# One weight sum earlier and four token sums one round later, at the end of an attention and two-layer kernel

## The chip, the cores and the metric

The kernel runs on one core of one Trainium2 chip. The metric is the device time of one execution in microseconds; the times given are medians over runs of the same program. TensorE (PE) multiplies, VectorE (DVE) and ScalarE (ACT) read its results out of the accumulator banks and work on them, GpSimd (POOL) masks and issues loads, SyncE (SP) issues stores and transposing transfers. Each engine takes its own instructions in the order in which the program lists them.

## What is computed

The reference first does causal attention, with 16 beacon keys and values ahead of the sequence, and then a two-layer block with a leaky ReLU between:

```python
B, H, S, Nb, D = (8, 8, 576, 16, 64)
n_tokens, d_model, d_ff = (4608, 512, 2048)
...
scores = scale * np.matmul(q, k_all.transpose(0, 1, 3, 2))   # k_all: beacon_k, then k
scores = np.where(causal, -1000000000.0, scores)
a = np.exp(scores - scores.max(-1, keepdims=True))
a /= a.sum(-1, keepdims=True) + 1e-09
attn_out = np.matmul(a, v_all)
...
x = attn_out.transpose(0, 2, 1, 3).reshape(B * S, H * D)
h = x @ w_in
g = np.maximum(0.01 * h, h)
return (g @ w_out).astype(np.float32)
```

## The kernel before

**Tiling.** The 4608 tokens are nine chunks of 512, numbered 0 to 8. The first layer of a chunk makes 16 blocks of 128 features (`up`, through `moe1`, line 442: four matmuls of 128x512 into one bank, then one ACT activation, line 450, into `gT`). The second layer is made by `down` (line 544). From chunk 1 on it is split in seven products over quarters of the operands instead of eight (Strassen's scheme in Winograd's form): products 1, 4, 6, 2, 7, 5, 3 in this order, each in two `down` steps of eight matmuls of 128x256. Products 5, 6 and 3 need sums over `gT`, which `token_sums` lists: four DVE additions for every four features, s1, s2, the overwritten quarter a21, and s4. DVE does them in `add_due` (line 784).

**The last two chunks.** When attention runs out of work, chunks 7 and 8 make a part of their first layer by seven products too. `in_round` makes four of the 16 blocks: products 1, 2, 6, 5, 4, 7, 3 (line 663, four matmuls of 128x256 each), with one `down` of the chunk behind it after product 1, after 5 and after 3. Product 1 and product 2 share a bank: ACT copies it after product 1 (line 697, called the p1 copy here), and product 2 then adds into the same bank. ACT copies product 5 in the same way (line 709). DVE combines (lines 706, 717, 718, 720, 721), and three activations, the leaves (line 680), wait in the list `leaves` for the results of lines 718, 720 and 721. `leave_all` issues them in the next round, one after its p1 copy, one after its product 2, one after its product 5, or all at once where it is called without a number. Weight sums for these products (`w_in_sums`) and sums over the tokens' columns (`x_in_sums`) are DVE work also.

**What sets the order.** The order is written out by hand. Nothing moves an instruction on its engine except the order in which the code calls it. DVE's sums go through a list, `due`: `add_due()` takes one off the front, and `up` and `down` each call it once. What a step leaves in the list is done at a later step. At the end of the attention part the list holds the rest of the weight sums and the token sums of chunk 6. `last_chunks` then takes the steps of a string one by one. `D` puts the list aside, does two `down`s and puts the list back. `X31` turns the last head pair, `x7` and `x8` make the column sums (two at once, two into the list at its third place), `R111` is an `in_round` with three `down`s, `t` issues all leaves and lists the token sums of the first four features, `u` is `leave_all` and `up`, `d` is `down`, `w` lists the last weight sums.

The steps for chunk 7 are `D X31 x7 d a1 R111 x8 R111 t u d u d u d u u d u d u u w`, those for chunk 8 `R111 R111 t R111 u d u d u d u d d d14`.

**Buffers.** The accumulators of the rounds and of `up` rotate through four banks (`ps_one`, named acc), those of `down` in this stage through two (`ps_sc`, named sc).

Of the kernel before, what the change touches and what calls it, by code (L numbers as in the profile page):

```python
# [15 lines left out]
def kernel(  # L16
# [383 lines left out]
    def x_transposes(g, copy):  # L400
        b, hp = divmod(g, NPAIR)
        x_nat, _ = xs.pop(g)
        ps = ps_one.tile([128, 1024], BF16, name="tp", tag="one")
        for t, (q0, rows) in enumerate(QT):
            nc.tensor.transpose(
                ps[:, q0 : q0 + rows],
                x_nat[0:rows, t].rearrange("p e d -> p (e d)"),
                ident[0:rows, 0:rows],
            )
        copy(out=xT[:, hp, x_at(b) : x_at(b) + S], in_=ps[:, 0:S])  # L410
# [20 lines left out]
    def moe1(i, fc):  # L431
        if i not in gT:
            gT[i] = gpool.tile([128, NF, 512], BF16, name="gT")
        acc = ps_one.tile([128, 512], FP32, name="acc", tag="one")
        at = i * 512 % (XR * S)
        cut = min(512, XR * S - at)
        for lo, hi in ((0, cut), (cut, 512)):
            for j in range(NJ):
                if lo == hi:
                    continue  # L440
                x0 = (at + lo) % (XR * S)
                nc.tensor.matmul(  # L442
                    out=acc[:, lo:hi],
                    lhsT=w_in_cols(fc, j),
                    rhs=xT[:, j, x0 : x0 + hi - lo],
                    start=(j == 0),
                    stop=(j == NJ - 1),
                    skip_group_check=True,
                )
        nc.scalar.activation(out=gT[i][:, fc, :], in_=acc, func=AF.Prelu, alpha=0.01)  # L450
# [25 lines left out]
    def token_sums(i, lo, hi):  # L476
        if i not in sums:
            sums[i] = [sum_tile(n).rearrange("p (c t) -> p c t", c=HF) for n in range(3)]
        g, s = gT[i], sums[i]
        a11, a12 = g[:, lo:hi, 0:HT], g[:, HF + lo : HF + hi, 0:HT]  # L480
        a21, a22 = g[:, lo:hi, HT : 2 * HT], g[:, HF + lo : HF + hi, HT : 2 * HT]
        s1, s2, s4 = (s[n][:, lo:hi] for n in range(3))
        return [
            dict(out=s1, in0=a21, in1=a22, op=ADD),
            dict(out=s2, in0=s1, in1=a11, op=SUB),
            dict(out=a21, in0=a11, in1=a21, op=SUB),
            dict(out=s4, in0=a12, in1=s2, op=SUB),
        ]
# [70 lines left out]
    def add_late(now=False):  # L559
        while late and (now or late[0][0] < done1[0] + done2[0]):  # L560
            late.pop(0)[1]()
# [57 lines left out]
    def w_in_sums(n, lo=0, hi=ROUNDS, first=False):  # L619
        cols = slice(lo * 256, hi * 256)  # L620
        (b11, b21), (b12, b22) = (
            [w_in_sb[i][:, at : at + 2, cols] for at in (0, 2)] for i in range(2)
        )
        x, y = {5: (b12, b11), 6: (b22, w_t[5][:, :, cols]), 4: (b21, w_t[6][:, :, cols]), 7: (b22, b12)}[n]
        at = 0 if first else len(due)
        due[at:at] = [
            (TAIL - 1, dict(out=w_t[n][:, j, cols], in0=x[:, j], in1=y[:, j], op=SUB)) for j in range(2)
        ]
# [8 lines left out]
    def x_in_sums(i):  # L637
        (a11, a12), (a21, a22) = x_parts(i)
        s1, s2, s3, s4 = (
            flat_a[t][:, lo : lo + X_COLS].rearrange("p (j t) -> p j t", j=2)  # L640
            for t, lo in sum_at[4 * (i - TAIL) : 4 * (i - TAIL) + 4]
        )
        x_sums[i] = {5: s1, 6: s2, 7: s3, 3: s4}
        return [
            (i, dict(out=s1, in0=a21, in1=a22, op=ADD)),
            (i, dict(out=s2, in0=s1, in1=a11, op=SUB)),
            (i, dict(out=s4, in0=a12, in1=s2, op=SUB)),
            (i, dict(out=s3, in0=a11, in1=a21, op=SUB)),
        ]
# [24 lines left out]
    def leave_all(n=3):  # L674
        while leaves and n:
            leave(*leaves.pop(0))
            n -= 1
# [9 lines left out]
    def in_round(i, r, downs):  # L687
        if i not in gT:
            gT[i] = gpool.tile([128, NF, 512], BF16, name="gT")
        add = nc.vector.tensor_tensor  # L690

        def bank():
            return ps_one.tile([128, 512], FP32, name="acc", tag="one")

        one = bank()
        in_product(i, 1, r, one, True)
        nc.scalar.copy(out=temps["p1"], in_=one)
        leave_all(1)
        for _ in range(downs[0]):
            down()  # L700
        in_product(i, 2, r, one, False)
        leave(i, 2 * r, 0, one)
        leave_all(1)
        six = bank()
        in_product(i, 6, r, six, True)
        add(out=temps["u2"], in0=six, in1=temps["p1"], op=ADD)
        five = bank()
        in_product(i, 5, r, five, True)
        nc.scalar.copy(out=temps["p5"], in_=five)
        leave_all()  # L710
        for _ in range(downs[1]):
            down()
        four = bank()
        in_product(i, 4, r, four, True)
        seven = bank()
        in_product(i, 7, r, seven, True)
        add(out=temps["u3"], in0=seven, in1=temps["u2"], op=ADD)
        add(out=temps["c21"], in0=four, in1=temps["u3"], op=ADD)
        in_product(i, 3, r, five, False)
        add(out=temps["c12"], in0=five, in1=temps["u2"], op=ADD)  # L720
        add(out=temps["c22"], in0=temps["u3"], in1=temps["p5"], op=ADD)
        leaves.extend(((i, 2 * r, 1, temps["c21"]), (i, HF + 2 * r, 0, temps["c12"]), (i, HF + 2 * r, 1, temps["c22"])))
        for _ in range(downs[2]):
            down()
        done1[0] += 4

    def last_chunks(steps):
        for step in steps.split():
            op, n = step[0], int(step[1:] or 1)
            i = done1[0] // NF  # L730
            if op == "d":
                for _ in range(n):
                    down()
            elif op == "u":
                for _ in range(n):
                    leave_all()
                    up()
            elif op == "R":
                in_round(i, done1[0] % NF // 4, [int(x) for x in step[1:]])
            elif op == "X":  # L740
                x_transposes(n, nc.vector.tensor_copy)
            elif op == "w":
                w_in_sums(7, ROUNDS - 1, ROUNDS)
            elif op == "x":
                x = x_in_sums(n)
                if n == TAIL:
                    for _, op in x[:2]:
                        nc.vector.tensor_tensor(**op)
                    due[2:2] = [x[3], x[2]]
                else:  # L750
                    due.extend(x)
            elif op == "a":
                add_due(n)
            elif op == "D":
                later = due[:]
                due.clear()
                down()
                down()
                due.extend(later)
            elif op == "t":  # L760
                leave_all()
                due.extend((i, op) for op in token_sums(i, 0, SLICE))
# [19 lines left out]
    def add_due(n=1):  # L782
        while due and n:
            nc.vector.tensor_tensor(**due.pop(0)[1])  # L784
            n -= 1
# [7 lines left out]
    def up():  # L793
        i1, n = divmod(done1[0], NF)
        assert i1 < ready[0]
        add_late()
        fc = n if i1 == 0 else n // 2 + n % 2 * HF
        moe1(i1, fc)
        if (i1, n) == (TAIL - 1, 4 * (ROUNDS - 1) + 2):
            w_in_sums(7, 0, ROUNDS - 1, first=True)  # L800
        add_due()
        done1[0] += 1
        turn[0] = 1
        if i1 and n % (2 * SLICE) == 2 * SLICE - 1:
            due.extend((i1, op) for op in token_sums(i1, n // 2 + 1 - SLICE, n // 2 + 1))

    def down():
        add_late()
        add_due()
        if at2[1] == 4:  # L810
            add_all(at2[0])
        moe2(*at2)
        done2[0] += 1
        at2[1] += 1
        if at2[1] == ND(at2[0]):
            at2[:] = at2[0] + 1, 0
        turn[0] = 0
# [94 lines left out]
    with order:  # L912
# [93 lines left out]
        assert at2 == [TAIL - 1, ND(TAIL - 1) - LEFT] and done1[0] == TAIL * NF, (at2, done1)  # L1006
        apart_from_values[0] = True
        last_chunks("D X31 x7 d a1 R111 x8 R111 t u d u d u d u u d u d u u w")
        last_chunks("R111 R111 t R111 u d u d u d u d d d14")


# [28 lines left out]
```

## Time and profile before

| what | value |
|---|---|
| median of 3 runs | 327.86 us (326.22 to 327.97) |
| time of the profiled execution | 328.3 us |
| its span, first to last instruction | 326.2 us |
| granted TensorE clock | 1.000 |
| busy: PE, DVE, ACT, POOL | 314.7, 168.2, 204.3, 184.4 us |
| last group of masks on POOL | up to 247.6 us |
| the string for chunk 7 begins with its first `down` | at 257.4 us |
| the first round of chunk 8 begins | at 284.0 us |
| last 128 matmuls, all of `down` | from 308.7 us |

Times of instructions are us from the start of the span. A row of the timeline gives the start, the time for which the instructions of the row were busy, engine, line, what is written and what is read, and the count. In brackets stands how long the engine sat idle before and what it then waited for. A row of several matmuls ends later than the next one starts, since the end of a matmul overlaps the next; so the pace of PE is read from start to start. Eight matmuls of 128x256 take 0.87 us in that way.

### The profile page before, as it was taken

The page shows a single profiled execution, that of the slowest core. Times are in us where ns is not written, and L with a number is a line of the kernel's source. Part 1 is how long each engine was busy: PE and PEld are TensorE (multiplying, and loading weights), DVE is VectorE, ACT ScalarE, POOL GpSimd, SP SyncE. Part 2 cuts the span into 40 slices and gives each one's busy share as a digit, 9 for nine tenths or more (in the row PEclk, how much of TensorE's full clock was granted, in tenths as well). Part 3 has the DMA queues.
Part 4 walks back from the last instruction along what each step waited for, and adds up shares of the span by engine and source line. Part 5 has one row for each costly group of instructions (what it writes and reads, how often), then busy time and mean ns, then how long its engine had stood idle before and what let it go on. Part 6 is the DMA issues. An engine that isn't in the chain of part 4 may idle for free.

```text
span 326.2 us, 8700 instructions
## 1 busy us (share of the span) xinstructions
PE 314.7 (96%) x3468; PEld 218.9 (67%) x3494; DVE 168.2 (52%) x341; ACT 204.3 (63%) x346; POOL 184.4 (57%) x354
## 2 busy tenths in 40 slices
PE   7999999999999999999999999999999989998995
PEld 4575555445688558845888888646865777687784
DVE  3473245508356145434553455345454689577754
ACT  4968962488765786478647873786477446564510
POOL 8795868989997687659875977674221000000000
PEclk9999999999999999999999999999999999999999
DMA  8999999999999999999999999999112100200113
GB/s 132 133 195 187 127 215 135 167 156 213 142 146 167 220 136 123 104 191 71 143 173 193 110 131 110 194 135 124 52 52 81 23 2 32 98 1 2 64 66 129
DMA packets 155256, 39.78 MB, mean 122 GB/s; under 512 B 142368, under 2 KB 152480, under 8 KB 155216
## 3 DMA queue, kind: packets, MB, share of 16 engines
q0 software_dynamic: 99824, 18.54, 88.6%
q1 hardware_dynamic: 55120, 20.62, 37.4%
q8 instruction: 27, 0.44, 0.6%
q14 instruction: 13, 0.11, 0.1%
q10 hardware_dynamic: 272, 0.07, 0.1%
HBM read 37.22 MB, written 9.44 MB: 143 GB/s over the span
## 4 chain that ended last, share of the span: by engine, by line
PE 76%; DMA 13%; ACT 4%; POOL 3%; issue 1%; DVE 1%; SPq 0%; ACTq 0%; DVEq 0%
PE acc L442 25%; PE acc L544 19%; PE sc L544 11%; PE av L359 7%; PE sc L314 6%; DMA gsum<-in_k_dram 5%; PE acc L663 4%; DMA w_out_sb<-in_moe_w_out_dram 4%; DMA kT<-k_nat 3%; ACT aT L333 2%; DMA k_nat<-in_k_dram 2%; PE sc L267 1%; POOL aT L289 1%; PE av L823 1%; ACT aT L276 1%
## 5 line engine op out<-in xcount | busy, mean ns | idle before, releaser
L442 PE MATMUL acc<-xT,w_in_sb 128*128 128x512 bf16 (+1 forms) x537 | 116.5, 354 | 1.6 <-ACT aT L329 0.3
L450 ACT ACTIVATE gT<-acc 128x512 bf16<-128x512 f32 x124 | 70.9, 623 | 33.2 <-PE acc L442 32.6
L289 POOL TENSOR_SCALAR_AFFINE_SELECT aT<-aT 128x256 bf16<-128x256 bf16 (+2 forms) x160 | 59.5, 403 | 50.5 <-ACT aT L329 30.9
L442 PEld LDWEIGHTS <-w_in_sb 128*128 128x128 bf16 x560 | 51.7, 98 | 44.0 <-issue 3.0
L544 PEld LDWEIGHTS <-gT 128*128 128x128 bf16 x512 | 48.8, 98 | 7.6 <-issue 1.6
L333 ACT ACTIVATE aT<-sc 128x1024 bf16<-128x1024 f32 (+3 forms) x64 | 51.7, 891 | 0.0
L329 ACT ACTIVATE aT<-sc 128x512 bf16<-128x512 f32 (+3 forms) x64 | 29.0, 520 | 27.5 <-PE sc L314 26.7
L388 DVE RECIPROCAL rec<-av 128x6 f32<-128x6 f32 (+1 forms) x64 | 12.0, 187 | 64.5 <-PE av L359 63.9
L359 PEld LDWEIGHTS <-aT 128*128 128x128 bf16 (+1 forms) x960 | 36.9, 98 | 9.0 <-issue 1.0
L544 PEld LDWEIGHTS <-gsum 128*128 128x128 bf16 x384 | 36.4, 98 | 7.7 <-DVE gsum L784 1.2
L359 PE MATMUL av<-v_aug,aT 128*128 128x65 bf16 (+1 forms) x960 | 39.7, 194 | 0.7 <-POOL aT L289 0.3
L214 POOL DMA_DIRECT2D v_aug<-in_v_dram x40 | 34.2, 858 | 4.1 <-DMA w_in_sb<-in_moe_w_in_dram 3.5
L171 POOL DMA_DIRECT2D k_nat<-in_k_dram x48 | 34.8, 732 | 1.9 <-DMA q_nat<-in_q_dram 0.7
L171 POOL DMA_DIRECT2D q_nat<-in_q_dram x48 | 34.8, 730 | 0.5 <-issue 0.3
L389 DVE TENSOR_TENSOR x_nat<-av,rec 128x384 bf16<-128x384 f32 (+1 forms) x64 | 31.4, 491 | 2.2
L544 PE MATMUL acc<-w_out_sb,gT 128*128 128x256 bf16 x240 | 28.9, 273 | 0.4 <-ACT gT L450 0.4
L276 ACT ACTIVATE aT<-sc 128x1024 bf16<-128x1024 f32 (+3 forms) x32 | 25.9, 871 | 4.3 <-PE sc L267 2.2
L314 PE MATMUL sc<-qT,kT 64*128 64x80 bf16 (+22 forms) x384 | 22.1, 250 | 0.2 <-DMA kT<-k_nat 0.2
L314 PEld LDWEIGHTS <-kT 64*128 64x128 bf16 x384 | 12.7, 94 | 11.1 <-issue 7.7
L544 PE MATMUL acc<-w_sum,gsum 128*128 128x256 bf16 x160 | 20.1, 273 | 0.0
L575 ACT COPY p<-acc 128x512 f32<-128x512 f32 x15 | 9.1, 604 | 16.8 <-PE acc L544 16.8
L784 DVE TENSOR_TENSOR gsum<-gT 128x1024 bf16<-128x1024 bf16 x16 | 11.3, 704 | 16.0 <-ACT gT L450 16.0
(95 smaller groups left out, 339.7 us busy)
## 6 DMA issues: line engine op xcount, KB each, us to landing
out_dram<-p SPq DMA_DIRECT2D x26, 256.0 KB, 3.6
q_nat<-in_q_dram POOLq DMA_DIRECT2D x48, 72.0 KB, 5.6
k_nat<-in_k_dram POOLq DMA_DIRECT2D x48, 72.0 KB, 5.0
v_aug<-in_v_dram POOLq DMA_DIRECT2D x24, 128.0 KB, 6.6
w_in_sb<-in_moe_w_in_dram POOLq DMA_DIRECT2D x2, 1024.0 KB, 12.1
w_out_sb<-in_moe_w_out_dram POOLq DMA_DIRECT2D x2, 1024.0 KB, 12.2
out_dram<-u SPq DMA_DIRECT2D x8, 256.0 KB, 2.7
gsum<-in_q_dram POOLq DMA_DIRECT2D x8, 144.0 KB, 7.1
```

Of the source, the lines that this page charges most:

```text
L171: nc.gpsimd.dma_start(out=t[:, :, par], in_=(q, k)[which][b, 2 * hp + par].rearrange("(t p) d -> p t d", p=NR),)
L214: nc.gpsimd.dma_start(out=dst[lo : ROWS[c], c, :, 0:D], in_=v[b, :, OFF[c] : OFF[c] + n].rearrange("h p d -> p h d"),)
L276: nc.scalar.activation(out=aT[:, :, c0 : c0 + w], in_=sc[:, :, 0:w], func=AF.Exp, scale=0.125)
L289: nc.gpsimd.affine_select(out=view, in_=view, compare_op=ALU.is_ge, fill=0.0, base=128 - n if lo == 0 else 0, channel_multiplier=-1, patte ...
L314: nc.tensor.matmul(out=(sc[par] if apart else sc[:, par])[:, at : at + b - a], lhsT=kT[ps_, c * 128 : (c + 1) * 128], rhs=qT[ps_, q0 : q0 ...
L329: nc.scalar.activation(out=probs[g][:, par, lo:hi], in_=sc[par][:, at : at + hi - lo], func=AF.Exp, scale=0.125)
L333: nc.scalar.activation(out=probs[g][:, :, lo:hi], in_=sc[:, :, at : at + hi - lo], func=AF.Exp, scale=0.125)
L359: nc.tensor.matmul(out=avv[:, n, 0 : D + 1], lhsT=aT[0 : ROWS[c], par, a0 : a0 + 128], rhs=va[0 : ROWS[c], c, 2 * hp + par, :], start=(c = ...
L389: nc.vector.tensor_tensor(out=x_nat[:, t0:t1].rearrange("p t e d -> p (t e) d"), in0=avv[:, :, 0:D], in1=rec[:, n0:n1, None].to_broadcast( ...
L442: nc.tensor.matmul(out=acc[:, lo:hi], lhsT=w_in_cols(fc, j), rhs=xT[:, j, x0 : x0 + hi - lo], start=(j == 0), stop=(j == NJ - 1), skip_gro ...
L450: nc.scalar.activation(out=gT[i][:, fc, :], in_=acc, func=AF.Prelu, alpha=0.01)
L544: nc.tensor.matmul(out=acc[:, lo : lo + HD], lhsT=left(i, n, fc, tile), rhs=right(n, fc), start=(lo == 0 and fc == 0), stop=(fc == HF - 1) ...
```

## The change

Two places. Inside `up`, at one block of chunk 6 (the one whose call lists the weight sums for product 7 ahead of everything), two sums are taken off the list instead of one. In the string for chunk 8, `t` stands after the third round instead of after the second. An assertion states that the list which `D` puts aside has four entries.

```diff
             elif op == "D":
                 later = due[:]
+                assert len(later) == 4, len(later)
                 due.clear()
                 down()
                 down()
...
         if (i1, n) == (TAIL - 1, 4 * (ROUNDS - 1) + 2):
             w_in_sums(7, 0, ROUNDS - 1, first=True)
+            add_due()
         add_due()
...
         last_chunks("D X31 x7 d a1 R111 x8 R111 t u d u d u d u u d u d u u w")
-        last_chunks("R111 R111 t R111 u d u d u d u d d d14")
+        last_chunks("R111 R111 R111 t u d u d u d u d d d14")
```

## Prediction

> **What bounds the kernel.** I read first the busy times and the chain of work that ended last, then the waits of PE, then the busy time by stage.
>
> ```profile
> PE 314.7 (96%) x3468; PEld 218.9 (67%) x3494; DVE 168.2 (52%) x341; ACT 204.3 (63%) x346; POOL 184.4 (57%) x354
> ...
> PE 76%; DMA 13%; ACT 4%; POOL 3%; issue 1%; DVE 1%; SPq 0%; ACTq 0%; DVEq 0%
> ```
>
> PE is busy for 96% of the span and holds 76% of the chain. Only the end matters here, since the change touches nothing ahead of 250 us. The waits of PE from 240 us to the end are two in all (waiter, what it waited for, total, times, longest):
>
> ```profile
> PE acc L663 <- ACT kT L697: 1.3, 1, 1.3
> PE sc L544 <- DVE gsum L784: 0.9, 1, 0.9
> ```
>
> Elsewhere in those 86 us PE waits for nobody, at a granted clock of 1.00. So the end is set by PE's list of matmuls plus these two gaps. Both lie at what the diff touches.
>
> The first gap, PE and then DVE:
>
> ```profile
> 262.47 0.60 PE L663 MATMUL acc<-aT 128*128 128x256 bf16 x4
> 262.91 0.60 PE L544 MATMUL sc<-w_sum,gsum 128*128 128x256 bf16 x4
> 264.43 0.61 PE L544 MATMUL sc<-w_sum,gsum 128*128 128x256 bf16 x4 [0.92 <-DVE gsum L784]
> ```
>
> ```profile
> 260.56 0.42 DVE L748 TENSOR_TENSOR aT<-aT,xT 128x512 bf16<-128x512 bf16 x1
> 260.91 0.55 DVE L784 TENSOR_TENSOR aT<-w_in_sb,aT 128x768 bf16<-128x768 bf16 x1
> 261.38 0.68 DVE L784 TENSOR_TENSOR gsum<-gT 128x1024 bf16<-128x1024 bf16 x1
> 261.98 0.42 DVE L784 TENSOR_TENSOR aT<-xT 128x512 bf16<-128x512 bf16 x1
> 262.74 0.69 DVE L706 TENSOR_TENSOR kT<-acc,kT 128x512 f32<-128x512 f32 x1 [0.35 <-PE acc L663]
> 263.35 0.42 DVE L784 TENSOR_TENSOR aT<-xT,aT 128x512 bf16<-128x512 bf16 x1
> 263.69 0.69 DVE L784 TENSOR_TENSOR gsum<-gsum,gT 128x1024 bf16<-128x1024 bf16 x1
> ```
>
> Product 6 of chunk 6 has its first four operands, but the other four are s2 of the last features, which DVE makes at 263.69 to 264.38. Ahead of it stand a weight sum (260.91), s1 (261.38), two column sums and line 706, which itself waits for PE.
>
> The second gap, PE and then ACT, in the third round of chunk 8:
>
> ```profile
> 295.38 0.60 PE L663 MATMUL acc<-xT,w_in_sb 128*128 128x256 bf16 x4
> 295.81 1.04 PE L544 MATMUL sc<-w_out_sb,gT 128*128 128x256 bf16 x8
> 298.14 0.60 PE L663 MATMUL acc<-xT,w_in_sb 128*128 128x256 bf16 x4 [1.29 <-ACT kT L697]
> ```
>
> ```profile
> 295.79 0.63 ACT L680 ACTIVATE gT<-aT 128x512 bf16<-128x512 f32 x1 [1.84 <-DVE aT L718]
> 296.39 0.63 ACT L680 ACTIVATE gT<-kT 128x512 bf16<-128x512 f32 x1
> 296.99 0.63 ACT L680 ACTIVATE gT<-aT 128x512 bf16<-128x512 f32 x1
> 297.52 0.57 ACT L697 COPY kT<-acc 128x512 f32<-128x512 f32 x1
> ```
>
> Product 1 ends at 295.98, and its copy could start there. But `t` put the three leaves of the second round ahead of the copy, and the first of them waits for DVE until 295.79. The copy ends at 298.09, and product 2 starts at 298.14.
>
> **The change, part by part.** No matmul, activation, addition or transfer is added or taken away. The instruction order of the changed kernel shows PE's, POOL's and SP's lists unchanged. So every DMA issue keeps its place; only DVE and ACT are reordered.
>
> *The second `add_due` in `up`.* The second half of the product 7 weight sum (0.41 us, at 252.93) moves ahead of a reciprocal, and everything after it in the list moves up one step. What remains for `D` is four token sums instead of five entries, and the weight sum at 260.91 now runs right behind its other half, at about 256.2. The list after `x7` becomes s1, s2, column sum, line 706, column sum, a21, s4. From the rows: the second L748 starts at 260.56, s1 takes its place at 260.91, s2 follows after a pace of 0.60 at 261.51 and ends at 262.20. PE wants it at 262.91 + 0.44 = 263.35. The margin is 1.15 us, so the gap goes. From start to start PE took 264.43 - 262.91 = 1.52 us for what takes 0.44: **1.08 us** off.
>
> What is late next there: product 7 of the round would end at 264.82, and line 717 behind a21 and s4 is free to start at 264.89, against 265.95 before, so DVE keeps up to within 0.1 us. The column sum for product 7 ends at 262.5 (wanted at 264.22), the one for product 3 at 263.8 (wanted at 264.65). Banks: product 6 of the next round needs the bank that line 720 frees, at about 266.97 against 267.72. All of them hold by 0.7 us or more, and behind them DVE's work follows PE's matmuls, so it shifts with them.
>
> What it costs: three moved sums now stand ahead of reciprocals. The weight sum ends at 251.75, the reciprocal behind it waits for PE until 252.37. s2 and a21 then run from 252.93 to 254.21, the next reciprocal starts at 254.46. s4 and two weight sums run from 255.17 to 256.79, the next at 257.61. The cover is idle DVE time, with 0.62, 0.25 and 0.82 us left. If it is gone, a reciprocal is late by at most one sum, 0.68 us. I cost it at nothing. Its bounds are 0 and 0.68.
>
> *`t` one round later.* ACT's order in the third round is now p1 copy, leave, leave of product 2, leave, p5 copy, leave. The copy starts at 296.02, when product 1 has ended, since ACT is idle from 293.95, and ends at 296.61. PE's eight `down` matmuls started at 295.81, so product 2 is due at 296.68. The margin is thin, 0.07 us, but the second round has the same distance (copy 290.34 to 290.93, product 2 at 291.01) and shows no wait. PE took 298.14 - 295.81 = 2.33 us where 0.87 would do: **1.46 us** off. The copy's place is bounded by 296.02 and by 297.52, where it stood: a gain of 1.46 to 0. I take 1.46, as the second round is the nearest row.
>
> What is late next: the three leaves are spread over the round. p5's copy would start at about 298.35 behind a leave, and end at 298.95; product 3 adds into that bank at 299.73, a margin of 0.8. Lines 718, 720 and 721 write what the leaves read; the last leave ends near 299.5, line 721 starts near 301.9. On DVE, s1 and s2 (0.60 each) leave the place ahead of lines 706 and 717 and stand after line 721, ahead of the two additions of product 7 (305.13 and 305.85), and a21 and s4 go behind these, into DVE's idle 2.00 us at 306.5 to 308.5. So two sums stand ahead of those additions, as two did before, and they shift by the full 1.46. Chunk 8 needs s2 only at its product 6, at 313.82 on the old clock, and the second half of s2, whose place is unchanged, ends at 311.28. A loss is possible only if DVE were late by more than 2.76 us: the first addition ended at 305.82, and PE reuses its bank at 308.58.
>
> From 298.14 to the last matmul PE waits for nothing, and the last additions and stores follow from it, so what is won reaches the end. **Sum:** 1.08 + 1.46 = 2.54 us. The profiled execution took 328.3 us with a span of 326.2; that gives 325.8 and 323.7. It lies 0.4 us above the median of the runs, 327.86. From the median: 325.3 to 325.4. I say 325.4.
>
> *A rule against it.* In the stage from 284 to 299 us weight loads were busy 12.12 of 15 us and matmuls 13.71, the two gaps being the only waits of PE. The Trainium skill (Perfetto Trace Analysis, Identifying the Most-Contended Engine) says that matmul occupancy does not tell how near TensorE is to its limit, and that the busy share of weight loads does. By it the 67% that the profile has for weight loads leaves a third of PE's time free, and closing two gaps might be worth nothing: 327.9. The stage has 81% even with its gap, so I keep the sum.
>
> **Rivals.**
>
> *Only one gap closes.* For: 0.07 us at the copy, 0.1 us at line 717. Against: each has a like row without a wait. Only the first closed gives 327.86 - 1.08 = 326.8; only the second 326.4. Chance 0.15.
>
> *It doesn't do what it says.* Both gaps reappear a step later, because DVE (17.43 of 22 us busy from 262 to 284) sets the pace of the rounds, not PE. Then 327.9. Against: DVE still shows idle time before line 717 in the rounds of chunk 8. Chance 0.05.
>
> *Slower.* The weight sum moved ahead of the reciprocal at 252.37 overwrites weights that PE reads. If it had to wait for the matmuls of `up` then running, until 257.0, the reciprocal, the product behind it and SP's three transposing transfers of head pair 30 (issued from 253.15 to 256.93, some 2.4 us to land) would be 4.7 us late. They land near 259.3, the first column sum needs them at 260.11: 0.8 us is covered, 3.9 is not. Less the 2.54 won, that is 1.4 more on the end, and with the accumulator banks held meanwhile some 0.3 to 0.6 more: about 329.7. It decides from a start later than 252.4 + 0.8. Against: its first half runs at 250.99 with no idle time before it, on the same columns. Chance 0.06.
>
> **How the numbers follow.** Both gaps closed 0.74, at 325.4; one 0.15; neither 0.05; slower 0.06. About 0.5%, 1.64 us, is what a measurement can tell from no change: below 326.2 is faster. Only the full case reaches that: 0.74. One gap or none is the same: 0.20. Slower: 0.06. The range goes from 324.0 (2.5 off the lowest run, 326.22, is 323.7, which a median will hardly reach) to 327.0 (only the first gap closed, and 0.2 for the reciprocals).
>
> **What would show it.** Right: no wait of PE for L784 or L697 after 250 us; s2 about 2.2 us earlier, straight behind s1; the p1 copy of chunk 8's third round within 0.1 us of its product 1; span near 323.7. Wrong: PE waits for L697, L706 or L717 in a round; reciprocals after 250 us that wait for DVE's own queue; a wait of the last `down`s for gsum.

## The result and the profile after

The changed kernel takes 325.65 us, the median of 10 runs (324.01 to 326.92), against 327.57 us for 10 runs of the kernel before (326.22 to 328.5). The ratio is 0.9941, with a 95% interval of 0.9917 to 0.9964: 1.9 us less, between 1.2 and 2.7. The profiled execution has a span of 323.8 us, against 326.2. In the repeats below some executions of each kernel took 1.5 to 3% longer than its fastest one, and the ratios leave these out.

From the page of the kernel after, the busy times and the chain that ended last:

```profile
PE 314.3 (97%) x3468; PEld 219.1 (68%) x3494; DVE 168.0 (52%) x341; ACT 203.8 (63%) x346; POOL 184.3 (57%) x354
...
PE 72%; DMA 14%; POOL 9%; ACT 3%; issue 1%; DVE 0%; POOLq 0%; ACTq 0%; SPq 0%
```

No engine's busy time changes by more than 0.5 us; PE is busy for the same 314 us in a shorter span. The waits of PE from 238 us to the end are an empty list now. The stage in which the second gap lay, the rounds of chunk 8, shows it too (stretch, its length, busy us with counts for PE, PEld, DVE, ACT and POOL, granted clock, DMA share, GB/s), first of the kernel before, then of the kernel after:

```profile
284.00:299.00 15.00, 13.71 (x125) 12.12 (x124) 10.54 (x18) 8.99 (x17) 0.00 (x0) 1.00 0.06 19
```

```profile
284.00:299.00 15.00, 15.00 (x140) 13.43 (x138) 11.22 (x20) 8.88 (x17) 0.00 (x0) 1.00 0.01 2
```

In the same 15 us PE gets 140 matmuls done instead of 125, and it is busy all the time.

Where the first gap was, PE and then DVE of the kernel after:

```profile
262.54 0.60 PE L663 MATMUL acc<-aT 128*128 128x256 bf16 x4
262.98 1.04 PE L544 MATMUL sc<-w_sum,gsum 128*128 128x256 bf16 x8
263.85 0.60 PE L663 MATMUL acc<-xT,aT 128*128 128x256 bf16 x4
```

```profile
260.63 0.42 DVE L748 TENSOR_TENSOR aT<-aT,xT 128x512 bf16<-128x512 bf16 x1
260.97 0.68 DVE L785 TENSOR_TENSOR gsum<-gT 128x1024 bf16<-128x1024 bf16 x1
261.69 0.69 DVE L785 TENSOR_TENSOR gsum<-gsum,gT 128x1024 bf16<-128x1024 bf16 x1
262.30 0.42 DVE L785 TENSOR_TENSOR aT<-xT 128x512 bf16<-128x512 bf16 x1
262.81 0.69 DVE L706 TENSOR_TENSOR kT<-acc,kT 128x512 f32<-128x512 f32 x1
```

The eight matmuls of chunk 6's product 6 run as one row of eight, with no bracket. The weight sum is gone from behind line 748, and s2 ends at 262.38, a microsecond before its four matmuls.

Where the second gap was, in the third round of chunk 8, PE and then ACT:

```profile
294.35 0.60 PE L663 MATMUL acc<-xT,w_in_sb 128*128 128x256 bf16 x4
294.79 1.04 PE L544 MATMUL sc<-w_out_sb,gT 128*128 128x256 bf16 x8
295.66 0.60 PE L663 MATMUL acc<-xT,w_in_sb 128*128 128x256 bf16 x4
```

```profile
294.99 0.59 ACT L697 COPY kT<-acc 128x512 f32<-128x512 f32 x1 [2.06 <-PE acc L663]
295.47 0.63 ACT L680 ACTIVATE gT<-aT 128x512 bf16<-128x512 f32 x1
```

Product 1 ends at 294.95, the p1 copy starts 0.04 us later, and the first leave follows it instead of leading it. Product 2 starts 0.87 us after the `down` in front of it, which is that step's own length.

### The profile page after: what moved, and what is told of

Its sections match the earlier page's. It is cut to its first block, busy times and chain, and to the rows that moved or that the text cites. A ratio compares the mean times of both kernels' runs of the same rounds, so it can differ in the third digit from the quotient of the medians.

```text
span 323.8 us, 8701 instructions
## 1 busy us (share of the span) xinstructions
PE 314.3 (97%) x3468; PEld 219.1 (68%) x3494; DVE 168.0 (52%) x341; ACT 203.8 (63%) x346; POOL 184.3 (57%) x354
## 4 chain that ended last, share of the span: by engine, by line
PE 72%; DMA 14%; POOL 9%; ACT 3%; issue 1%; DVE 0%; POOLq 0%; ACTq 0%; SPq 0%
PE acc L442 24%; PE acc L544 19%; PE sc L544 11%; PE av L359 6%; PE sc L314 5%; PE acc L663 5%; DMA w_out_sb<-in_moe_w_out_dram 4%; DMA gsum<-in_k_dram 4%; POOL aT L289 3%; DMA k_nat<-in_k_dram 3%; DMA v_aug<-in_v_dram 2%; ACT aT L333 2%; DMA kT<-k_nat 2%; POOL gsum L158 1%; POOL v_aug L214 1%
```

## The experiments

The work ahead of 257 us does not take the same time in every profile. The changed kernel, profiled twice, began the last group of value matmuls (line 359) at 256.92 and at 255.08 us. That is 1.84 us with the same program, nearly as much as the change itself. So for every trace I also take the **tail**: from the start of that group to the start of the last row of 16 `down` matmuls. Before it is 320.88 - 256.85 = 64.03 us; after it is 318.40 - 256.92 = 61.48. The sums that the first part moves run ahead of this stretch, so what they might cost there is read from the rows around them instead (below, at the idle DVE time).

My theory is that of the prediction: PE's own list of matmuls sets the end from 257 us on, and two waits, each with a cause of its own, were taken out of it. The rivals are one common cause, token sums that get in the way elsewhere, and DVE as the pace of the rounds.

| label | what it is | ratio to before (95%) | tail, us | against before |
|---|---|---|---|---|
| after | both parts | 0.9941 (0.9917 to 0.9964) | 61.48 | -2.55 |
| e3_after_again | both parts, once more | 0.9927 (0.9901 to 0.9953) | 61.48 | -2.55 |
| e1_sum_only | the weight sum alone | 0.9971 (0.9944 to 0.9999) | 62.93 | -1.10 |
| e2_t_only | the later `t` alone | 0.9953 (0.9933 to 0.9973) | 62.57 | -1.46 |
| e4_leaves3 | after, three leaves early | one profile | 62.93 | -1.10 |
| e5_leaves1 | after, one leaf early | one profile | 61.73 | -2.30 |
| e6_leaves2 | after, two leaves early | one profile | 62.34 | -1.69 |
| e7_dup2 | after, two sums more on DVE | one profile | 61.59 | -2.44 |
| e8_dup4 | after, four sums more on DVE | one profile | 62.77 | -1.26 |

### The two halves and the whole

The whole is the changed kernel itself. The halves take one part each:

```diff
 e1_sum_only, against the kernel after
-        last_chunks("R111 R111 R111 t u d u d u d u d d d14")
+        last_chunks("R111 R111 t R111 u d u d u d u d d d14")
 e2_t_only, against the kernel before
-        last_chunks("R111 R111 t R111 u d u d u d u d d d14")
+        last_chunks("R111 R111 R111 t u d u d u d u d d d14")
```

> The changed kernel once more, on the same chip as its two halves. Theory (PE's list of matmuls sets the end, two gaps closed): no wait of PE after 240 us, 2.5 us less than before, ratio 0.992. Rival (the gaps come back later, or the reciprocals pay): a ratio nearer to 0.996, with waits of PE somewhere after 250 us.

> Only the second weight sum in up; the token sums of chunk 8 asked for after the second round, as before. Theory: the wait of 0.92 us for the token sum near 264 us is gone, the wait of 1.29 us for the p1 copy stays at its full size; span 1.08 us shorter (ratio 0.9967). Rival (the wait for the copy is a matter of DVE being late from the first gap on, so both go with one cause): the second wait shrinks too, 2 us or more off.

> Only the token sums of chunk 8 asked for after the third round; up takes one weight sum as before. Theory: the wait for the p1 copy is gone, the wait of 0.92 us near 264 us stays; 1.46 us off (ratio 0.9955). Rival (the sums now land on the additions of product 7): a wait of PE for line 572 or for gsum after 300 us, and less than 1 us off.

The waits of PE from 240 us on are, for e1 and then for e2 (waiter, what it waited for, total us, times, longest):

```profile
PE acc L663 <- ACT kT L697: 1.3, 1, 1.3
```

```profile
PE sc L544 <- DVE gsum L784: 0.9, 1, 0.9
```

Each half leaves the other's wait in place and unchanged, and the whole has none. The tails are 1.10 and 1.46 us shorter, 2.56 together, and the whole is 2.55 shorter. The ratios say the same with wider intervals: 0.29% and 0.47% make 0.76%, and the whole measured 0.73% in the same comparison and 0.59% in the first one. So the waits are independent, the rival of one common cause falls, and so does that of token sums which land on the additions of product 7: e2 has no wait of PE after 300 us.

### Which of the two things that `t` does

`t` issues the leaves on ACT and lists the token sums for DVE. A step `l` of its own issues leaves alone, before the third round, while the sums stay after it:

```diff
+            elif op == "l":
+                leave_all(n)
...
-        last_chunks("R111 R111 R111 t u d u d u d u d d d14")
+        last_chunks("R111 R111 l3 R111 t u d u d u d u d d d14")
```

e5 has `l1` and e6 `l2` in its place.

> The changed kernel, but all three leaves of the second round are issued ahead of the third, as before; the token sums stay after the third round. Theory (the copy stood behind the leaves on ACT): product 2 of the third round starts 1.46 us late again, as before the change. Rival (the token sums on DVE ahead of lines 706 and 717 made the gap): no wait there, since the sums are still late.

> The changed kernel with one of the three leaves issued ahead of the third round. Theory: that leave waits for line 718, which ends at 294.73 in the profile of the changed kernel; it runs to 295.4, the p1 copy from 295.3 to 295.9, and product 2 starts at about 295.94 where 295.66 was due: 0.28 us late. Rival (DVE's token sums made the gap): 0.

> The changed kernel with two of the three leaves issued ahead of the third round. Theory: the second waits for line 720, which ends at 295.32; the p1 copy runs from 295.9 to 296.48, and product 2 starts at about 296.53 instead of 295.66: 0.87 us late. Rival (DVE's token sums): 0.

ACT in the third round, first of e5, then of e6:

```profile
294.68 0.63 ACT L680 ACTIVATE gT<-aT 128x512 bf16<-128x512 f32 x1 [1.84 <-DVE aT L718]
295.21 0.57 ACT L697 COPY kT<-acc 128x512 f32<-128x512 f32 x1
```

```profile
294.68 0.63 ACT L680 ACTIVATE gT<-aT 128x512 bf16<-128x512 f32 x1 [1.84 <-DVE aT L718]
295.28 0.63 ACT L680 ACTIVATE gT<-kT 128x512 bf16<-128x512 f32 x1
295.82 0.57 ACT L697 COPY kT<-acc 128x512 f32<-128x512 f32 x1
```

With none, one, two and three leaves ahead of the copy the tail is 61.48, 61.73, 62.34 and 62.93 us: 0, 0.25, 0.86 and 1.45 us more, where 0, 0.28, 0.87 and 1.46 were expected. The first leaf costs little, since its wait for line 718 ends just before the copy could have begun: it starts at 294.68 in e5, where product 1 ends at 294.86. Each further one costs its own pace, 0.60 us. The rival, DVE's token sums, gave 0 for all three, and falls: these sums stand in their new place in all of them. Besides, e4 and e1 differ only in the place of these sums and have the same tail, 62.93 us, so with the leaves in front the place of the sums is worth nothing. The other case, the sums early and the leaves late, was not run; whether the sums had to move as well is therefore not shown.

### More work for DVE at the first gap

The last half of the weight sum for product 4 is made again, to the same values, ahead of s1. This is the edit of e7; e8 has `range(4)`:

```diff
                     for _, op in x[:2]:
                         nc.vector.tensor_tensor(**op)
+                    cols = slice(0, ROUNDS * 256)
+                    for _ in range(2):
+                        nc.vector.tensor_tensor(
+                            out=w_t[4][:, 1, cols], in0=w_in_sb[0][:, 3, cols], in1=w_t[6][:, 1, cols], op=SUB
+                        )
```

> The changed kernel with the last weight sum made twice more, to the same values, right behind the two column sums of line 748: 0.94 us more for DVE ahead of s1 and s2. Theory (PE's list is the bound, DVE has a margin of about 1.1 us at s2 and 0.75 us at the bank that line 720 frees): no wait for gsum, product 6 of the next round 0.1 to 0.2 us late, so 0.1 to 0.2 us on the end. Rival (DVE sets the pace of the rounds): the 0.94 us go to the end in full.

> The same with four more weight sums, 1.88 us for DVE. Theory: s2 ends at about 264.3 instead of 262.4 and product 6 of chunk 6 waits some 0.9 us; behind it 0.1 to 0.2 us more at the bank that line 720 frees; 1.0 to 1.1 us on the end. Rival (DVE sets the pace): 1.88 us on the end.

PE of e8, and then three DVE rows of it:

```profile
262.70 0.60 PE L544 MATMUL sc<-w_sum,gsum 128*128 128x256 bf16 x4
264.41 0.61 PE L544 MATMUL sc<-w_sum,gsum 128*128 128x256 bf16 x4 [1.12 <-DVE gsum L790]
```

```profile
260.69 2.33 DVE L751 TENSOR_TENSOR aT<-w_in_sb,aT 128x768 bf16<-128x768 bf16 x4
262.94 0.69 DVE L790 TENSOR_TENSOR gsum<-gT 128x1024 bf16<-128x1024 bf16 x1
263.66 0.69 DVE L790 TENSOR_TENSOR gsum<-gsum,gT 128x1024 bf16<-128x1024 bf16 x1
```

The wait that the change removed is back, between the fourth and the fifth matmul of chunk 6's product 6. The four sums took 262.94 - 260.69 = 2.25 us of DVE's time, not the 1.88 expected, and the two of e7 1.06 us. The tails grew by 1.29 and 0.11 us. In e8 this product 6 lost 264.41 - 262.70 - 0.44 = 1.27 us, in e7 0.10. So about 1.0 us of DVE time is free at this place, and only what goes beyond it reaches the end. The rival, DVE as the pace of the rounds, asked for all 2.25 us and all 1.06, and falls for this place.

What was off was twofold. The repeated sums cost more than I counted. And the further 0.1 to 0.2 us did not come at the round's own product 6, which was said to need the bank that line 720 frees. In e8 these are the row of line 720 and the rows of products 2 and 6 of the next round:

```profile
268.14 0.68 DVE L720 TENSOR_TENSOR kT<-acc,kT 128x512 f32<-128x512 f32 x1
```

```profile
268.35 0.60 PE L663 MATMUL acc<-xT,w_in_sb 128*128 128x256 bf16 x4
268.79 0.60 PE L663 MATMUL acc<-aT,aT 128*128 128x256 bf16 x4
```

Product 6 starts on pace, 0.44 us after product 2, and 0.03 us before line 720 is shown to end (268.82). In e7 it is the same, 267.69 against 267.72. The matmuls that did wait for DVE here started after its sum had ended, 264.41 against 264.35 in e8. So product 6 did not wait for line 720, and the traces speak against the reading that it needs that bank. Which bank comes late next stays open.

## Why the prediction was right

The forecast was 325.4 us, and the median is 325.65. That the two lie so close is in part luck. The forecast started from 327.86, the median of three runs; ten runs of the kernel before gave 327.57, and 2.54 us less than that is 325.03. The steps of the forecast are better judged one by one:

- **What bounds the kernel.** PE's list with two gaps in it. Shown: the halves close one gap each, and the gains add up. The doubts that the busy share of weight loads raised did not come true. (The stage that was read for them holds only the second of the two gaps; the first lies near 264 us.) In the stage from 284 to 299 us matmuls are now busy 15.00 of 15 us and weight loads 13.43, that is 90%. A weight load takes 98 ns there and a matmul of 128x256 starts every 109 ns (eight in 0.87 us), so 90% is what a full PE shows with this shape. With 128x512, where four matmuls take 0.87 us, 216 ns each, the same load would fill only 45%, an estimate from these two times. The 68% of the whole profile mixes such shapes, so it does not mean that a third of PE's time was to spare.
- **First gap.** 1.08 us predicted, 1.10 measured. s2 was put at 261.51; it came at 261.69, of which 0.07 us come from the later start of the last value matmuls (256.92 against 256.85) and the rest from s2, which follows s1 at 0.72 us, not at the pace of 0.60 taken; it reads what s1 writes. The margin at chunk 6's product 6 was 1.04 us where 1.15 was said; e7 and e8 measured about the same.
- **Idle DVE time as cover for the moved sums.** 0.62, 0.25 and 0.82 us were to be left ahead of three reciprocals. The kernel after shows 0.62, 0.26 and 0.82 (the first row is the weight sum that the slower rival was about):

```profile
251.06 0.75 DVE L785 TENSOR_TENSOR w_in_sb<-w_in_sb 128x512 bf16<-128x512 bf16 x2
252.43 0.18 DVE L388 RECIPROCAL rec<-av 128x4 f32<-128x4 f32 x1 [0.62 <-PE av L359]
...
254.53 0.20 DVE L388 RECIPROCAL rec<-av 128x6 f32<-128x6 f32 x1 [0.26 <-PE av L359]
...
257.67 0.18 DVE L388 RECIPROCAL rec<-av 128x4 f32<-128x4 f32 x1 [0.82 <-PE av L359]
```

  All three reciprocals still wait for PE, and from 240 to 262 us PE is busy for 21.84 us in both kernels. Nothing was paid there. The rival that ended slower needed the moved weight sum to start after 253.2; it ran straight behind its other half and was done by 251.81.
- **Second gap.** 1.46 us predicted, 1.46 measured. The thin margin held: the copy ended at 295.58 and product 2 started at 295.66. The p5 copy was said to start at 298.35. That was counted in the times of the trace before, and the third round begins 1.03 us earlier in the trace after (294.35 against 295.38), so 297.32 is to be compared; it started at 297.31.
- **Reaching the end.** Nothing was given back. The tails show 2.55 us for the 2.54 predicted.
- **The size in the runs.** The medians give 1.9 us, and the 2.54 of the forecast lie inside the interval of 1.2 to 2.7; the second comparison gave 0.9927, which is 2.4 us. What makes the 0.6 us between 1.9 and 2.54 is not shown. The tail does not show it, since it is 61.48 us in both profiles, and the ten runs of the changed kernel alone spread over 2.9 us.
- **A side step that was wrong.** Product 6 of the next round as waiting for the bank of line 720, and so as what is late next. It decided nothing in the sum; in e7 and e8 product 6 started before line 720 had ended.

## What to carry to other kernels

When one engine is full but for two named waits, as here, the gain of a reordering is the sum of the two, each read from start to start and not from the bracket, if every instruction that slips has idle time behind it that is longer than its slip. In a queue that works in order, an instruction that frees a bank for the busy engine belongs ahead of instructions that wait for a third engine; here the first instruction in front of it cost 0.25 us, and each further one its full pace of 0.60. And where the rest of the program varies as much as the change is worth, compare the traces from a common point onward before judging a median.

## What the runs showed of the hardware that was not expected

In these traces a DVE addition that overwrites what the one before it wrote starts later behind it than an independent one of the same shape: the row of four 128x768 sums in e8 is 2.33 us long, 0.59 us from start to start, while the two halves of that sum in the kernel after, which write different columns, are 1.02 us together, 0.47 us apart. s2, which reads what s1 wrote, also starts later: 0.72 us behind s1, against 0.60 for independent sums of 128x1024, a21 and s4.
